# Clamping nine weight pieces in PSUM, one unit's maximum later, and the first batch's value products on half rows

## The chip, the cores and the metric

One core of a Trainium2 chip runs the whole program. The metric is the device time of one execution in microseconds (us), the median of several runs. One of the runs is taken with the hardware profiler, and all rows below come from that execution. TensorE is called PE, VectorE DVE, ScalarE ACT, GpSimd POOL, and the queue that issues the transfers SP.

## The reference

The program computes an attention with 32 memory slots per head and then two expert layers, all in fp32:

```python
# batch 8, heads 8, seq 576, head_dim 64, n_mem 32
a    = softmax(phi, axis=slots)                      # (b, h, s, 32)
k_m  = einsum('bhsm,bhsd->bhmd', a, k)
v_m  = einsum('bhsm,bhsd->bhmd', a, v)
attn = softmax(q @ k_m.T / 8)                        # (b, h, s, 32)
x    = (attn @ v_m) as 4608 tokens x 512
h    = x @ w_in;  g = max(0.01*h, h);  x = g @ w_out             # w_in 512x2048, w_out 2048x512
y    = sigmoid(x @ w_gate) * (x @ w_val) @ w2_out                # 512x1536 twice, 1536x512
```

The first expert's weights w_in and w_out, and the second's, arrive as float64 words; the kernel turns each word into a float32 itself. "Piece" is 128 x 512 such words.

## The kernel before, in words

Since `x @ w_in` is `attn @ (v_m @ w_in)`, the kernel never forms x. For each batch it builds the product of v_m and w_in (tile `vw`), in eight blocks of 256 columns, split in a high and a low half for three-pass fp32 products. The main loop then runs over (batch, half of the tokens, block of 128 hidden columns): a "step". In a step i, in the order in which instructions are written for every engine (an order by hand, with in-order queues):

1. `fin`: the high part (`gh`, ACT) and the low part (`gl`, POOL, for a few steps of the list `gldve` DVE) of the activation of step i+1.
2. `m1_in` of step i+2 (L801): six products on PE into a bank `ps_h`, then the activation `gr` on ACT (L818).
3. The vector parts `v...` of the attention units that are due, interleaved in rounds with `tick`s. If a `vw` block was multiplied in step i-1, its split (`done`, ACT copy and DVE subtraction) comes in front.
4. The PE parts `t...` of the units.
5. If due (`vw0`: steps 2, 5, 8, 13, 20, 22), the PE products of one more `vw` block of batch 0 (`vw_block`, L760).
6. `m1_out` of step i (L824): twelve products into four banks `acc`.

A unit is half of a batch's heads (two per batch). Its parts run in a chain: v1 the slots' maximum over tokens (L472), t1 a PE transpose, v2 the maximum over it (tile `mx`), t2 a product that spreads it, v3 exp input, v4 sums, t4 `ps_kv` (k_m and v_m), v5 their scaling (r on DVE, then tile `e` on ACT, L580), t5 transposes, v6 the copy to `kvT` (ACT, L607), t8 scores, v8 transposes (DVE, L635), v9 to v11 the softmax and its split into `at_hi` and `at_lo`. The list `chain1` gives for each part its step, counted from the unit's start: units of batch 1 start at steps 1 and 13. All PE parts of units and of `vw` blocks share one pool of two PSUM banks, `ps_a`, used in turn; a bank is given out again when the instructions that read it are done. PSUM is full: four banks `acc`, two `ps_h`, two `ps_a`.

The weights of the first expert are converted by ticks. Tick n starts piece n-1 (`a`: y, k and the sign, three ACT instructions), adds for piece n-4 (`c`, POOL), clamps piece n-2 (`b`, DVE, L226), shifts and xors piece n-3 (`b2`, DVE, L234), and stores piece n-5 (`d`: for w_out a split by ACT and POOL). A block of w_in is two pieces. `y` has five SBUF buffers, `k` four. `done_until(n)` runs ticks until piece n has passed.

Before the loop a prologue, written as a list of groups, runs the two units of batch 0, the first maximum of the third unit (`v1.2`) and twelve ticks (`T`); then the first two `vw` blocks are multiplied and split one after the other. Unit 0 and 1 of batch 0 keep zeros in the other unit's 64 rows of `kvT` (their scale is a column of a mask), so `vw_block` multiplies all 128 rows and adds both units' columns in one bank. From batch 1 on `vw_pair` (L777) multiplies only the unit's own 64 rows, of two blocks at once, one bank per unit.

After the first expert (703 us) the second expert runs on PE without a break to the end.

Of the kernel before, what the change touches and what calls it, by code (L numbers as in the profile page):

```python
# [8 lines left out]
F32 = mybir.dt.float32  # L9
F32R = mybir.dt.float32r  # L10
I32 = mybir.dt.int32
# [6 lines left out]

SCHED = {'vw0': [2, 5, 8, 13, 20, 22],
# [5 lines left out]
 'ticks': [1, 1, 1, 1, 2, 1, 1, 2, 0, 1, 0, 1, 1, 2, 0, 0, 0, 1, 1, 1, 1, 1, 0, 0, 1, 0, 0, 0, 0, 0],  # L27
 'lopool': [0, 1, 2, 3, 4, 5, 6, 7, 8, 9, 10, 11, 12, 13, 14],
 'gldve': [3, 4, 6, 12, 26, 31],
 'upool': ['v10.1', 'v10.2', 'v10.3', 'v11.0', 'v11.1', 'v11.2', 'v11.3', 'v9.0', 'v9.2', 'v9.3'],  # L30
# [63 lines left out]
            'lq1': 0,  # L94
            'lq2': 1,
            'lq3': 2,
            'v1': -5,
            't1': -1,
            'v2': 0,
            't2': 1,  # L100
            'v3': 3,
            'v3e': 3,
            'v4': 4,
# [15 lines left out]
def tile_kernel(  # L119
# [13 lines left out]
    nc = tc.nc  # L133
    P = 128
    B, H, S, D = q.shape
    M = phi.shape[3]
# [6 lines left out]
    HG = 4  # L143
    NG = H // HG
# [4 lines left out]
    VB = 256  # L149
# [14 lines left out]
    cvp = p1.enter_context(tc.tile_pool(name="cvp", bufs=2))  # L164
    q, k, v, phi = (x.rearrange("b (h g) s d -> b g h s d", g=NG) for x in (q, k, v, phi))
    dr = ctx.enter_context(tc.tile_pool(name="dr", bufs=1, space=bass.MemoryType.DRAM))
    ps_acc = ctx.enter_context(tc.tile_pool(name="ps_acc", bufs=4, space=bass.MemoryType.PSUM))
# [11 lines left out]
    def f32(ap):  # L179
        return ap.bitcast(F32)  # L180

    def wtile(tag, shape, dt, name):
        return wp.tile(shape, dt, tag=tag, name=name, bufs=SLOTS[tag])

    def split(raw, hi, lo, eng=nc.vector):
        nc.scalar.copy(hi, raw)  # L186
        eng.tensor_sub(lo, raw, f32(hi))  # L187
# [7 lines left out]
    PC = 512  # L195

    class Piece:
        late = False

        def __init__(self, src, done, f_dst=None, raw=None):  # L200
            self.src, self.done, self.f_dst, self.raw = src, done, f_dst, raw
# [7 lines left out]

        def a(self):  # L210
            w = self.raw.rearrange("p (n t) -> p n t", t=2)
            self.y = cvp.tile([P, PC], F32, tag="y", name="y", bufs=5)
            self.k = cvp.tile([P, PC], F32, tag="k", name="k", bufs=4)
            nc.scalar.activation(self.y, w[:, :, 1].bitcast(F32), AF.Abs, scale=2.0 ** -3)
            nc.scalar.activation(self.k, w[:, :, 0], AF.Copy, scale=2.0 ** -27, bias=2.0 ** 25)
            if not self.late:
                self.sign()
            yield
# [11 lines left out]

        def b2(self):
            w = self.raw.rearrange("p (n t) -> p n t", t=2)
            yi = self.y.bitcast(I32)
            nc.vector.scalar_tensor_tensor(  # L234
                out=yi, in0=yi, scalar=3, in1=w[:, :, 1].bitcast(I32),
                op0=ALU.logical_shift_left, op1=ALU.bitwise_xor,
            )
            yield
# [10 lines left out]
    win = {}  # L249
# [24 lines left out]
    def wout_pieces(j):  # L274
        def done(c, f):
            if c == 0:
                stage["wo", j] = [wtile("wo", [P, 2, DM], F32R, "wo") for _ in range(2)]
            hi, lo = (t[:, c, :] for t in stage["wo", j])
            split(f, hi, lo, nc.gpsimd if 2 * j + c in SCHED["lopool"] else nc.vector)
            wout[2 * j + c] = (hi, lo)  # L280
# [6 lines left out]
    def stash_jobs():  # L287
# [12 lines left out]
        def prep(key, o0):  # L300
# [40 lines left out]
            def h(f, *a):  # L341
                return lambda: f(*a)
# [51 lines left out]
    kvT = {}  # L394
    vw = {}
# [68 lines left out]
    def unit_engine(part, u):  # L464
        return nc.gpsimd if u[0] > 1 or f"{part}.{u[0] * NG + u[1]}" in SCHED["upool"] else nc.vector

    def psa(name):
        return ps_a.tile([P, 512], F32, tag="a", name=name)
# [288 lines left out]
            PARTS[n + "ab"[i]] = lambda u, f=f, i=i: f(u, i)  # L757


    def vw_block(j):  # L760
        p = psa("ps_vw")
        for g in range(NG):
            for h in range(HG):
                nc.tensor.matmul(
                    p[M * h:M * h + M, g * VB:(g + 1) * VB],
                    kvT[0, g][:, 1, M * h:M * h + M], win[j][:, h, :], start=True, stop=True,
                )

        def done():
            t = vw[0, j] = wtile("vw", [P, 2, NG, VB], F32R, "vw")  # L770
            split(p.rearrange("p (g f) -> p g f", g=NG), t[:, 0], t[:, 1])
            yield

        return done


    def vw_pair(b, j0):  # L777
        js = (j0, j0 + 1)
        ps = [psa("ps_vw") for _ in range(NG)]
        for n, j in enumerate(js):  # L780
            for h in range(HG):
                for g in range(NG):
                    nc.tensor.matmul(  # L783
                        ps[g][M * h:M * h + M, n * VB:(n + 1) * VB],
                        kvT[b, g][D * g:D * g + D, 1, M * h:M * h + M],
                        win[j][D * g:D * g + D, h, :], start=True, stop=True,
                    )
        for j in js:
            vw[b, j] = wtile("vw", [P, 2, NG, VB], F32R, "vw")
        for g in range(NG):  # L790
            ws = [(ps[g][:, n * VB:(n + 1) * VB], vw[b, j]) for n, j in enumerate(js)]
            for x, w in ws:
                nc.scalar.copy(w[:, 0, g], x)
            for x, w in ws:
                nc.vector.tensor_sub(w[:, 1, g], x, f32(w[:, 0, g]))  # L795

    hps = {}
    gt = {}
    acc = {}

    def m1_in(b, hf, fc):  # L801
# [17 lines left out]
        gt[b, hf, fc] = (gh, gl)  # L819
        return lambda: split(gr, gh, gl, nc.vector if b == 0 and hf * NF + fc in SCHED["gldve"] else nc.gpsimd)  # L820

    BEGIN = [sum(SCHED["groups"][:i]) for i in range(len(SCHED["groups"]) + 1)]

# [264 lines left out]
    with tc.manual_schedule():  # L1088
# [8 lines left out]
        pieces = []  # L1097
        pos = [0]
        for j in range(NVB):
            pieces += win_pieces(j) + wout_pieces(j)  # L1100
        n_start = len(pieces)

        raws = iter(pieces)

# [8 lines left out]
        def run(gens):  # L1113
            gens = list(gens)
            while gens:
                gens = [g for g in gens if next(g, gens) is not gens]

        def chain(gens):
            for g in gens:
                yield from g  # L1120
# [30 lines left out]
        def done_until(n):  # L1151
            while pos[0] < n + 5:
                run([tick()])
# [3 lines left out]

        U0 = dict(zip(units[2:], SCHED["units"]))
        for b in range(3, B):
            for g in range(NG):  # L1160
                U0[b, g] = (b - 1) * NS + SCHED["unit"][g]
        VW_AT = {b: [(b - 1) * NS + x for x in SCHED["vw"]] for b in range(3, B)}
# [13 lines left out]
        def first_vw(j):  # L1176
            done_until(4 * j + 2)
            return vw_block(j)

        def unit_parts(i):  # L1180
            vs, ts_, ls = [], [], []
            for u, u0 in U0.items():
                parts = [n for n, k in SCHED[{1: "chain1", 2: "chain2"}.get(u[0], "chain")].items() if k == i - u0]
                v = [PARTS[n](u) for n in parts if n[0] == "v"]
                if v:
                    vs.append(chain(v))
                ts_ += [(PARTS[n], u) for n in parts if n[0] == "t"]
                ls += [
                    (PARTS[n], u) for n in parts
                    if n[0] == "l" and u not in units[:3]  # L1190
                ]
            return vs, ts_, ls
# [6 lines left out]
            else:  # L1199
                (unit_phi, unit_kv, unit_q)["pkq".index(x[0])](units[int(x[1])])  # L1200
        waiting = []
        n_vw = n_in = 0
        fin = None
        for group in SCHED["prologue"]:
            vs, ts_ = {}, []
            for n, f in enumerate(waiting):
                vs["w", n] = [f()]
            waiting = []
            for x in group.split():
                if x == "T":  # L1210
                    vs.setdefault("T", []).append(tick())
                elif x == "W":
                    ts_.append(None)
                else:
                    n, u = x.split(".")
                    u = units[int(u)]
                    if n[0] == "v":
                        vs.setdefault(u, []).append(PARTS[n](u))
                    else:
                        ts_.append((PARTS[n], u))  # L1220
            run([chain(v) for v in vs.values()])
            for t in ts_:
                if t:
                    t[0](t[1])
                else:
                    waiting.append(first_vw(n_vw))
                    n_vw += 1
        run([f() for f in waiting])
        while n_vw < 2:
            run([first_vw(n_vw)()])  # L1230
            n_vw += 1
        for i in range(LA):
            fin = step_in(*steps[i])
            if i + 1 < LA:
# [67 lines left out]
        for n in range(len(PAIRS)):  # L1302
            more = n + 1 < len(PAIRS)
            for th in range(NTH):
                for j in range(TH // 2):
                    for val in range(2):
                        g = m2_group(n, th, j, val)
                        if (n, th, j, val) == (0, 0, 0, 0):
                            g = first
# [49 lines left out]
```

## Time and profile before

| what | value |
|---|---|
| device time, median of 3 runs | 1602.17 us (1600.76 to 8618.76) |
| the profiled execution's own time | 1601.75 us |
| its span, first to last instruction | 1599.9 us |
| PE busy | 1549.1 us, 97% |
| DVE, ACT, POOL busy | 827.7, 707.9, 431.0 us |
| mean granted clock of PE | 0.989 |

The span is 1.85 us shorter than the time of the same execution. Busy shares are means over the span; in the slices of the page PE shows 5 to 7 tenths in the first two of forty slices (40 us each) and 9 in nearly all others. The changed code runs in the first 145 us.

### The profile page before, as it was taken

The numbers are of one execution on the slowest core, as the hardware profiler recorded it, in microseconds if no ns is written. First come the engines' busy times: TensorE is split into PE (matmuls) and PEld (weight loads), VectorE is DVE, ScalarE is ACT, GpSimd is POOL, SyncE is SP. The second block draws the span as 40 slices with busy tenths as digits, with TensorE's granted clock in tenths as the row PEclk, the third lists the DMA queues.
The fourth block names the chain that finished last, engine by engine and source line by source line (L and its number), as shares of the span: only waits on it lengthen the run. The fifth ranks groups of instructions, "written<-read, shape, count | busy, mean of one in ns | idle before, by whom it ended". The sixth has DMA issues, their size and how long they took to land.

```text
span 1599.9 us, 27447 instructions
## 1 busy us (share of the span) xinstructions
PE 1549.1 (97%) x10544; PEld 1358.0 (85%) x10544; DVE 827.7 (52%) x1426; ACT 707.9 (44%) x1602; POOL 431.0 (27%) x429
## 2 busy tenths in 40 slices
PE   5799999999999999999999999999999999999998
PEld 2677988999999998999988888888888888888898
DVE  6886444555554545422145474355545475255544
ACT  5885455565556555645333143223333143223332
POOL 3886343554445444543100020000200020000100
PEclk8799999999999999999999999999999999999999
DMA  9822554554556455322446446536546446536692
GB/s 306 277 53 64 160 143 138 150 154 139 159 146 192 140 160 146 115 82 97 146 170 218 140 156 234 191 115 222 195 163 222 141 150 236 169 109 223 223 398 76
DMA packets 203490, 268.66 MB, mean 168 GB/s; under 512 B 95072, under 2 KB 140128, under 8 KB 203360
## 3 DMA queue, kind: packets, MB, share of 16 engines
q1 hardware_dynamic: 203360, 266.92, 52.1%
q8 instruction: 83, 1.36, 0.4%
q14 instruction: 47, 0.39, 0.1%
HBM read 219.68 MB, written 47.19 MB: 167 GB/s over the span
## 4 chain that ended last, share of the span: by engine, by line
PE 82%; ACT 1%; DVE 1%; DMA 1%; issue 0%; POOL 0%; DVEq 0%; SPq 0%; ACTq 0%; POOLq 0%
PE acc L835 20%; PE oacc L1041 18%; PE ps_y L943 14%; PE ps_h L813 9%; PE ps_x L943 9%; PE ps_z L943 9%; PE ps_vw L783 1%; PE ps_kv L550 1%; DMA wt<-gvs 1%; PE ps_sc L625 0%; ACT gr L818 0%; ACT obuf L844 0%; DVE vw L795 0%; DVE t L530 0%; ACT raw L222 0%
## 5 line engine op out<-in xcount | busy, mean ns | idle before, releaser
L835 PE MATMUL acc<-gh,wo 128*128 128x288 f32 x2048 | 428.7, 301 | 3.7 <-ACT obuf L844 2.7
L835 PEld LDWEIGHTS acc<-gh,wo 128*128 128x128 f32 x2048 | 328.9, 189 | 28.4 <-issue 13.8
L835 PE MATMUL acc<-gl,wo 128*128 128x288 f32 x1024 | 304.8, 298 | 2.1 <-POOL gl L187 2.1
L187 POOL TENSOR_TENSOR gl<-gr,gh 128x288 fp32r<-128x288 f32 x250 | 215.6, 864 | 329.9 <-ACT gh L186 216.6
L1041 PE MATMUL oacc<-w2t,pt 128*128 128x512 f32 x1296 | 296.3, 389 | 0.0
L1041 PEld LDWEIGHTS oacc<-w2t,pt 128*128 128x128 f32 x1296 | 243.1, 188 | 50.3
L943 PE MATMUL ps_y<-xo,wt 128*128 128x512 f32 (+1 forms) x1080 | 251.9, 369 | 0.0
L813 PE MATMUL ps_h<-at_hi,vw 128*128 128x288 f32 x1024 | 214.6, 298 | 6.1 <-ACT vw L186 4.7
L943 PEld LDWEIGHTS ps_y<-xo,wt 128*128 128x128 f32 x1080 | 190.4, 188 | 33.8
L818 ACT ACTIVATE gr<-ps_h 128x288 f32<-128x288 f32 x256 | 105.7, 413 | 254.2 <-PE ps_h L813 226.1
L906 POOL TENSOR_TENSOR xo<-xr,xo 128x512 fp32r<-128x512 f32 (+1 forms) x16 | 23.0, 1460 | 671.0 <-ACT xo L902 671.0
L835 PEld LDWEIGHTS acc<-gl,wo 128*128 128x128 f32 x1024 | 193.7, 189 | 3.0 <-POOL gl L187 3.0
L813 PEld LDWEIGHTS ps_h<-at_hi,vw 128*128 128x128 f32 x1024 | 166.6, 190 | 7.5 <-ACT vw L186 5.6
L943 PE MATMUL ps_z<-xo,wt 128*128 128x512 f32 (+1 forms) x720 | 167.4, 368 | 0.6 <-DMA wt<-gvs 0.6
L943 PE MATMUL ps_x<-xo,wt 128*128 128x512 f32 (+1 forms) x720 | 167.5, 368 | 0.0
L813 PE MATMUL ps_h<-at_lo,vw 128*128 128x288 f32 x512 | 151.6, 296 | 0.0
L978 ACT CAST pt<-sg 128x512 fp32r<-128x512 f32 (+1 forms) x120 | 69.4, 578 | 182.0 <-DVE sg L971 182.0
L943 PEld LDWEIGHTS ps_z<-xo,wt 128*128 128x128 f32 x720 | 127.0, 189 | 23.1 <-DVE tmp L1024 0.7
L943 PEld LDWEIGHTS ps_x<-xo,wt 128*128 128x128 f32 x720 | 127.2, 188 | 22.9
L186 ACT CAST gh<-gr 128x288 fp32r<-128x288 f32 x256 | 111.8, 437 | 2.2
L813 PEld LDWEIGHTS ps_h<-at_lo,vw 128*128 128x128 f32 x512 | 97.2, 190 | 0.0
L990 ACT COPY tmp<-ps_x 128x512 f32<-128x512 f32 (+1 forms) x60 | 32.5, 542 | 136.6 <-PE ps_x L943 136.6
(171 smaller groups left out, 1719.0 us busy)
## 6 DMA issues: line engine op xcount, KB each, us to landing
wt<-gvs SPq DMA_DIRECT2D x210, 512.0 KB, 4.6
w2t<-w2s SPq DMA_DIRECT2D x60, 512.0 KB, 5.5
gvs<-hl SPq DMA_DIRECT2D x84, 256.0 KB, 2.4
x2s<-obuf SPq DMA_DIRECT2D x15, 576.0 KB, 3.7
win<-in_moe_w_in_dram SPq DMA_DIRECT2D x16, 512.0 KB, 9.8
wo_bits<-in_moe_w_out_dram SPq DMA_DIRECT2D x16, 512.0 KB, 10.4
xr<-x2s SPq DMA_DIRECT2D x16, 512.0 KB, 6.2
out_dram<-osum SPq DMA_DIRECT2D x32, 256.0 KB, 2.0
```

The costliest lines, as they stand in the source:

```text
L186: nc.scalar.copy(hi, raw)
L187: eng.tensor_sub(lo, raw, f32(hi))
L550: nc.tensor.matmul(p[M * h:M * h + M, 0:2 * D], a, x, start=(c == 0), stop=(c == CC))
L783: nc.tensor.matmul(ps[g][M * h:M * h + M, n * VB:(n + 1) * VB], kvT[b, g][D * g:D * g + D, 1, M * h:M * h + M], win[j][D * g:D * g + D, h, ...
L813: nc.tensor.matmul(p[:, :HALF], w, x, start=(n == 0), stop=(n == 3 * NG - 1))
L818: nc.scalar.activation(gr, p[:, :HALF], AF.Prelu, alpha=0.01)
L835: nc.tensor.matmul(a[d][:, :HALF], w[:, ds_], x, start=(open_ and n == 0), stop=(close and n == 2),)
L906: eng.tensor_sub(t[:, 1, :h], x_operand(n, k, a), f32(t[:, 0, :h]))
L943: nc.tensor.matmul(bank, w[:, l, a, :], x[:, r, :h], start=(start and i == 0), stop=(i == 5), skip_group_check=not start,)
L978: nc.scalar.copy(d[:, 0, :h], s)
L990: read(lambda: nc.scalar.copy(s1, x))
L1041: nc.tensor.matmul(bank[i], pt[2 * f + t][:, l, q * P:(q + 1) * P], w2t[f][:, r, :], start=(f == 0 and l + r == 0), stop=(f == TH - 1 and ...
```

## The change

There are four edits. (1) For pieces 0 to 8 the tile y, which ACT writes and DVE clamps, lies in a PSUM bank of the `acc` pool; the shift and xor reads it there and writes an SBUF tile. (2) Part v1 of the third unit (batch 1, first half) leaves the prologue: in `chain1` v1 now has step -1 (of the unit's start at 1 and 13), and t1, v2 and t2 move one step later. (3) `vw_block` multiplies 64 rows per unit, as `vw_pair` does, into two banks of `ps_a`; its split is two ACT copies and two DVE subtractions of 256 columns in place of one each of 512. (4) The first two blocks are multiplied together at `W`, before the last prologue group, and their split runs interleaved with that group. The block of step 13 moves to step 12.

```diff
-SCHED = {'vw0': [2, 5, 8, 13, 20, 22],
+SCHED = {'vw0': [2, 5, 8, 12, 20, 22],
...
-              'v9.0 v7a.1 T v4.1 v9e.0 t4.1', 't7b.1 T', 't5.1 v5.1 v7b.1', 'T v1.2', 'v10.0 T', 't8a.1 v6.1',
-              'v10t.0 t8b.1 T v8a.1', 'v11.0', 'v8b.1 v9.1 T', 'T T v9e.1 T v10.1 v10t.1 v11.1'],
+              'v9.0 v7a.1 T v4.1 v9e.0 t4.1', 't7b.1 T', 't5.1 v5.1 v7b.1', 'T', 'v10.0 T', 't8a.1 v6.1',
+              'v10t.0 t8b.1 T v8a.1', 'v11.0', 'v8b.1 v9.1 T', 'T T v9e.1 W', 'T v10.1 v10t.1 v11.1'],
+ 'banks': 9,
...
-            'v1': -5,
-            't1': -1,
-            'v2': 0,
-            't2': 1,
+            'v1': -1,
+            't1': 0,
+            'v2': 1,
+            't2': 2,
...
         def a(self):
-            self.y = cvp.tile([P, PC], F32, tag="y", name="y", bufs=5)
+            if self.bank:
+                self.y = ps_acc.tile([P, PC], F32, tag="acc", name="y_bank")
+            else:
+                self.y = cvp.tile([P, PC], F32, tag="y", name="y", bufs=5)
...
         def b2(self):
-            yi = self.y.bitcast(I32)
+            y = self.y
+            if self.bank:
+                self.y = cvp.tile([P, PC], F32, tag="y", name="y", bufs=5)
             nc.vector.scalar_tensor_tensor(
-                out=yi, in0=yi, scalar=3, in1=w[:, :, 1].bitcast(I32),
+                out=self.y.bitcast(I32), in0=y.bitcast(I32), scalar=3, in1=w[:, :, 1].bitcast(I32),
...
+    def vw_products(b, js):
         ps = [psa("ps_vw") for _ in range(NG)]
         for n, j in enumerate(js):
             for h in range(HG):
                 for g in range(NG):
                     nc.tensor.matmul(
                         ps[g][M * h:M * h + M, n * VB:(n + 1) * VB],
                         kvT[b, g][D * g:D * g + D, 1, M * h:M * h + M],
                         win[j][D * g:D * g + D, h, :], start=True, stop=True,
                     )
+        return ps
...
+    def vw_block(j):
+        ps = vw_products(0, (j,))
+        def done():
+            vw_tiles(0, (j,))
+            for part in ("hi", "lo"):
+                vw_split(part, 0, [(0, j)], ps, range(NG))
+                yield
+        return done
...
+        def first_vws():
+            done_until(6)
+            ps = vw_products(0, (0, 1))
+            def done():
+                vw_tiles(0, (0, 1))
+                for j in (0, 1):
+                    for part in ("hi", "lo"):
+                        vw_split(part, 0, [(j, j)], ps, range(NG))
+                        yield
+            return done
```

## Rows read from the trace of the kernel before

**Rows 1.** Stretches: start:end length, then busy PE PEld DVE ACT POOL, clock, DMA
```profile
40.00:50.00 10.00, 2.54 (x16) 0.71 (x16) 9.93 (x13) 7.01 (x13) 7.21 (x7) 0.60 1.06 371
80.00:90.00 10.00, 9.46 (x112) 7.69 (x110) 9.86 (x12) 8.45 (x19) 8.18 (x8) 1.00 0.54 135
400.00:1600.00 1200.00, 1192.15 (x7301) 1041.29 (x7299) 583.33 (x990) 461.20 (x1007) 214.09 (x217) 1.00 0.52 171
```

**Rows 2.** Timeline, end of the prologue: start, duration, engine, line, tiles, [idle before]
```profile
52.10 0.61 PE L813 MATMUL ps_h<-at_hi,vw 128*128 128x288 f32 x1 [0.70 <-DVE vw L187]
52.54 0.79 POOL L187 TENSOR_TENSOR at_lo<-atr,at_hi 128x288 fp32r<-128x288 f32 x1
```

**Rows 3.** Timeline of DVE and POOL in the prologue
```profile
31.74 0.41 DVE L226 TENSOR_SCALAR y<-y 128x512 f32<-128x512 f32 x1
50.86 1.72 POOL L187 TENSOR_TENSOR wo<-y,wo 128x512 fp32r<-128x512 f32 x1
51.37 1.28 DVE L187 TENSOR_TENSOR vw<-ps_vw,vw 128x512 fp32r<-128x512 f32 x2
```

**Rows 4.** DVE in 20 to 53 us, L226 alone, then L234 alone
```profile
20.00:53.00 33.00, 8.17 (x11) 0.68 1.07 366
...
20.00:53.00 33.00, 9.39 (x9) 0.68 1.07 366
```

**Rows 5.** Timeline of PE: products of a block, of a pair, and what follows
```profile
61.28 1.19 PE L764 MATMUL ps_vw<-win,kvT 128*32 128x256 f32 x16
62.40 0.54 PE L835 MATMUL acc<-gh,wo 128*128 128x288 f32 x2
227.20 1.09 PE L783 MATMUL ps_vw<-win,kvT 64*32 64x256 f32 x32
228.23 0.54 PE L835 MATMUL acc<-gh,wo 128*128 128x288 f32 x2
```

**Rows 6.** Timeline and stretches: a pair held at a bank, and the clock then
```profile
239.47 1.50 PE L783 MATMUL ps_vw<-win,kvT 64*32 64x256 f32 x30 [3.08 <-DVE mx L492]
...
241.00:243.00 2.00, 2.00 (x9) 2.00 (x10) 1.32 (x4) 1.52 (x5) 0.34 (x1) 0.50 0.80 261
```

**Rows 7.** Timeline, steps 2 to 4: DVE's `gl`, and PE's wait for `obuf`
```profile
63.04 1.30 DVE L187 TENSOR_TENSOR gl<-gr,gh 128x288 fp32r<-128x288 f32 x1 [0.18 <-ACT gh L186]
70.20 0.85 PE L835 MATMUL acc<-gh,wo 128*128 128x288 f32 x2 [2.73 <-ACT obuf L844]
```

**Rows 8.** Timeline, step 8: PE's block, DVE's r, ACT's scaling
```profile
85.46 1.53 PE L764 MATMUL ps_vw<-win,kvT 128*32 128x256 f32 x16
88.89 0.15 DVE L560 TENSOR_SCALAR r<-ps_kv 128x1 f32<-128x1 f32 x1
88.95 1.09 DVE L479 TENSOR_REDUCE t<-ph 128x128 f32<-128x512 f32 x1
90.16 0.47 ACT L580 ACTIVATE e<-ps_kv,r 128x256 f32<-128x256 f32 x1 [1.14 <-DVE r L562]
```

**Rows 9.** Timeline, step 23: the split in front of a PE part
```profile
138.11 0.41 ACT L818 ACTIVATE gr<-ps_h 128x288 f32<-128x288 f32 x1 [2.63 <-PE ps_h L813]
139.78 0.71 PE L625 MATMUL ps_sc<-qT,kvT 64*32 64x288 f32 x14 [1.16 <-DVE vw L187]
```

**Rows 10.** Timeline, steps 12 and 20: PE, and what a block there waits for
```profile
99.45 0.51 PE L835 MATMUL acc<-gh,wo 128*128 128x288 f32 x2
101.25 1.72 POOL L242 TENSOR_TENSOR win<-y,k 128x512 int32<-128x512 int32 x1
126.13 1.07 PE L764 MATMUL ps_vw<-win,kvT 128*32 128x256 f32 x16
130.15 0.45 ACT L580 ACTIVATE e<-ps_kv,r 128x256 f32<-128x256 f32 x1
```

**Rows 11.** Waits in 50 to 145 us: who for whom: us in total, times, longest
```profile
PE acc L835 <- POOL gl L187: 2.1, 3, 1.1
PE ps_kvT L595 <- ACT e L580: 1.4, 2, 0.9
```

More of the change, by code (lines that the diff above doesn't have):

```diff
@@ L197, in tile_kernel @@
     class Piece:
-        late = False
+        late = bank = False
         def __init__(self, src, done, f_dst=None, raw=None):
@@ L757, in tile_kernel @@
             PARTS[n + "ab"[i]] = lambda u, f=f, i=i: f(u, i)
[L760 to L778, printed above, removed]
+    def vw_products(b, js):
         ps = [psa("ps_vw") for _ in range(NG)]
@@ L787, in vw_pair, with vw_split, vw_tiles @@
                     )
+        return ps
+    def vw_split(part, b, js, ps, gs):
+        for g in gs:
+            for n, j in js:
+                x, w = ps[g][:, n * VB:(n + 1) * VB], vw[b, j]
+                if part == "hi":
+                    nc.scalar.copy(w[:, 0, g], x)
+                else:
+                    nc.vector.tensor_sub(w[:, 1, g], x, f32(w[:, 0, g]))
+    def vw_tiles(b, js):
         for j in js:
             vw[b, j] = wtile("vw", [P, 2, NG, VB], F32R, "vw")
-        for g in range(NG):
[L791 to L795, printed above, removed]
+    def vw_block(j):
[6 more added lines that the diff above has]
+        return done
+    def vw_pair(b, j0):
+        js = (j0, j0 + 1)
+        ps = vw_products(b, js)
+        vw_tiles(b, js)
+        for g in range(NG):
+            for part in ("hi", "lo"):
+                vw_split(part, b, list(enumerate(js)), ps, (g,))
     hps = {}
@@ L1101, in tile_kernel @@
         n_start = len(pieces)
+        for p in pieces[:SCHED["banks"]]:
+            p.bank = True
         raws = iter(pieces)
@@ L1178, in first_vw @@
             return vw_block(j)
+        def first_vws():
[4 more added lines that the diff above has]
+                for j in (0, 1):
+                    for part in ("hi", "lo"):
+                        vw_split(part, 0, [(j, j)], ps, range(NG))
+                        yield
+            return done
         def unit_parts(i):
@@ L1201, in tile_kernel @@
         waiting = []
-        n_vw = n_in = 0
         fin = None
@@ L1225, in tile_kernel @@
                 else:
[L1226 to L1231, printed above, removed]
+                    waiting.append(first_vws())
         for i in range(LA):
```

## The prediction

> **What bounds the kernel now.** I first read the stretches of the span [rows 1]. After 400 us PE is busy 1192 of 1200 us and nothing of the change runs there, so only the first 145 us can move. There two regimes follow each other. In 40 to 50 us DVE is busy 9.93 of 10 and PE 2.54 at a clock of 0.60: DVE sets the time at which PE can start the main loop. In 80 to 90 us PE is busy 9.46, but DVE 9.86: PE leads and DVE follows some microseconds behind, which costs nothing as long as PE has other work in front of what DVE owes it. Next I read the timeline at the border of the two [rows 2]: the first product in full flow starts at 52.10 (PE had waited for a low half from DVE), and POOL's last `at_lo` of the prologue, which the same products need, runs from 52.54. Then I read the waits of PE in the loop [rows 7, 11]: 2.73 us at 70.20 for `obuf`, 2.1 in three for POOL's `gl`, 1.4 in two for `e`. These are the waits that another delay of PE would swallow.
>
> **The prologue (edits 1, 2 and the pair).** DVE loses the maximum of the third unit, 1.09 by its like at 88.95 [rows 8], and its small second instruction: 1.3 us. It moves to step 0, where DVE waits for ACT before its next clamp; if that cover is gone it costs the same 1.3. The nine shift-and-xors take 9.39 us in all, 1.04 each [rows 4]. A subtraction of the same size with one operand in PSUM took 0.64 while POOL worked beside it (51.37, POOL from 50.86) [rows 3]; at that price nine cost 5.8, a gain of 3.6. The clamps: eleven take 8.17 [rows 4], so nine about 6.7, in proportion. No row shows a clamp in PSUM. One end is 0.41, the clamp in SBUF beside no POOL work [rows 3], nine for 3.7; the other is 0.64, nine for 5.8. I take 0.64, since its operand lies in PSUM as the changed clamp's does: a gain of 0.9 (at the other end 3.0). The Trainium skill, "VectorE: DVE Perf Modes", section "Why PSUM operands drop a tier", speaks against this edit: an fp32 operand in PSUM keeps DVE from its two-port mode. By that rule the clamp costs one element per cycle and the sum stays as it is; without it DVE would gain 2.1 us more.
>
> ACT's nine writes of y into PSUM have no row either. I take nothing, between one clamp's difference of 0.23 gained and as much lost for each.
>
> DVE is thus about 5.8 us shorter. What is late next is POOL: its queue keeps its order, and a store (1.72) and the multiplication of the softmax stand ahead of `at_lo` [rows 2, 3]. The new order even puts both splits and one more tick ahead of unit 1's sums on DVE. So between 0 and 5.8 I take **-2.0**: POOL's row at 52.54 lies close behind PE's release at 52.10, nearer to no gain than to all. The pair itself runs while PE has nothing else to do: 0. Transfers are issued in the same order: 0.
>
> **Products on half rows (edit 3).** An undisturbed block takes 61.28 to 62.40, 1.12; a pair of half-row blocks 227.20 to 228.23, 1.03, so 0.52 a block [rows 5]. Six blocks lie in the loop: 6 x 0.6 = **-3.6** (at least -2.4, if one block alone does not pipeline as a pair does and costs 0.72). The split in two costs ACT and DVE one fixed cost more each, which ACT's and DVE's idle time after 94 us hides; before that it counts in the lags below.
>
> **What edit 3 adds: two banks instead of one.** `ps_a` has two. A block now waits until both are read, and the unit's PE part of the next step waits until the block is split. PE is in order, so everything behind stands still. A pair shows this wait already: 3.08 us until DVE's maximum `mx`, and then a clock of 0.50, the lower of its two levels, for at least 2 us, which loses 1.0 us [rows 6].
> - Step 2: v2 now falls in this step, and DVE runs it behind `gl`, which ends at 64.34; with the maximum (0.3, estimated) 64.6. PE is there at 61.28: +3.3 [rows 5, 7].
> - Step 3: t2 waits for the split, which ACT runs behind the `gr` of the product that PE has just made. In step 23 the same order already costs 138.11 to 139.78, 1.67, of which 1.16 is idle [rows 9]; with halves of 256 columns I take +1.3. The wait at 70.20 is then paid: -2.73. Clock: one drop before and one after, 0.
> - Step 5: its readers ran a step earlier, 0.
> - Step 8: `e` ends at 90.63; without the other unit's maximum, which now is due in step 12, r's second instruction follows the first and `e` ends near 89.7. PE is there at 85.46 [rows 8]: 4.2, less 0.7 by which PE is late by then (3.3 + 1.3 - 2.73 - two blocks' 1.2): +3.5. The clock after it: +1.0. The later wait of t5 for the same `e` goes: -0.5 [rows 11].
> - Steps 9 and 13: the split in front of t5 and t1, +1.3 each.
> - Step 12: the block waits for a conversion that ends at 102.97, and stands where PE was at 99.45 [rows 10]: 3.5, but PE is 5.4 late by then, so 0.
> - The waits for `gl`: -2.1 [rows 11].
> - Step 20: `e` ends at 130.60, PE was there at 126.13 [rows 10]: 4.5; PE is 4.0 late: +0.5. Its t5's own wait: -0.9.
> - Step 21: +1.3. Steps 22 and 23 already have theirs: 0.
>
> Sum: 3.3 + 1.3 - 2.7 + 3.5 + 1.0 - 0.5 + 1.3 + 1.3 - 2.1 + 0.5 - 0.9 + 1.3 = +7.3. With -2.0 and -3.6: **+1.7 us**. Against the profiled execution's 1601.75 this is 1603.5; the median of the runs shown lies 0.4 above it, so I leave it at 1603.5.
>
> **Rivals.** *The gain is kept (0.30).* DVE, freed of POOL, keeps its lead into the loop, so that the readers of steps 2 and 8 come early. Then the start gives -4, the blocks -3.6, the two waits about 1 each, the four splits 5.2, and half of the 6.2 us of old waits is swallowed: -3.5, 1598. For it: DVE ends the prologue with little idle time [rows 1]. Against: what DVE follows at step 2 is ACT's `gh` (0.18 idle before 63.04 [rows 7]), and ACT loses no work.
>
> *The waits pile up, slower (0.15).* My zeros in steps 12 and 20 assume that the other engines do not wait for PE. But ACT's queue in each step stands behind the `gr` of a product that PE has just made, so when PE is late the reader may be as late. Then steps 12 and 20 pay their 3.5 and 4.5 in full with a clock drop each: +3.5 + 4.0 + 2.0 more, 1613. It decides from the point at which PE idles over 2 us ahead of the block's products in step 12. The Trainium skill, "TensorEngine Tiling (Array Packing)", section "Restrictions and Gotchas", names its root: different row tiles write to different banks, so row tiling raises the pressure on PSUM. No run here shows yet what that costs a single block.
>
> *The first edits do nothing (0.05):* POOL holds the start where it is. Then +3.7, 1605.5.
>
> My forecast, even within some microseconds (1599 to 1607), has 0.50.
>
> **The numbers.** 1595 to 1611 leaves out the ends of the two large rivals, about 0.2. The forecast's own range is 1599 to 1607. 2%, about what a measurement of this kernel can tell from no change, is 32 us. No case reaches that: all PE waits of the first 60 us together would be needed for a gain, and three times the pile-up for a loss. So faster 0.01, same 0.97, slower 0.02.
>
> **What would show it.** Start: the first product in full flow near 50, not 52.1; shift-and-xor of the first nine pieces at 0.64 whatever POOL does; clamps at 0.64. Blocks: 0.5 to 0.6 of PE each. Waits: idle time of PE ahead of the block's products in step 2 (for `mx`) and step 8 (for `e`), some 3 us each, with the clock at 0.50 behind, and 1 us ahead of t2, t5 and t1; no wait at `obuf`. I am wrong if PE reaches the products of step 8 with `e` already done (faster), or if step 12 or 20 idles as long as step 8 (slower).

## The result and the profile after

The changed kernel takes 1619.34 us (median of 4 runs, 1616.80 to 1620.36), against 1601.74 for the kernel before in the same runs: ratio 1.0110, 95% interval 1.0090 to 1.0129. It is slower by about 1.1%, and above the range given. The profiled execution took 1616.80, 15.05 more than that of before (1601.75); its span is 1615.0.

| | before | after |
|---|---|---|
| span, us | 1599.9 | 1615.0 |
| PE busy, us | 1549.1 | 1551.4 |
| DVE, ACT, POOL busy, us | 827.7, 707.9, 431.0 | 818.8, 708.0, 428.2 |
| mean granted clock of PE | 0.989 | 0.987 |

DVE is indeed relieved of 9 us and PE works nearly as long as before: the loss is idle time of PE. The stretches that answer to [rows 1] (start:end length, busy PE, PEld, DVE, ACT, POOL, clock, DMA):

```profile
40.00:50.00 10.00, 3.46 (x19) 1.18 (x19) 7.12 (x14) 6.89 (x14) 7.75 (x7) 0.50 1.06 374
80.00:90.00 10.00, 5.63 (x77) 4.43 (x75) 8.39 (x12) 8.80 (x21) 8.52 (x7) 1.00 0.59 141
400.00:1600.00 1200.00, 1195.29 (x7391) 1045.72 (x7390) 586.99 (x992) 466.11 (x1022) 220.53 (x224) 1.00 0.52 171
```

In 80 to 90 us PE falls from 9.46 to 5.63. After 400 us PE is about as busy as before. The waits of PE in 50 to 145 us, which answer to [rows 11] (who for whom: us in total, times, longest):

```profile
PE ps_vw L771 <- ACT e L586: 7.1, 2, 4.8
PE ps_h L826 <- ACT at_hi L187: 5.2, 1, 5.2
PE ps_vw L771 <- POOL win L248: 3.4, 2, 2.7
PE ps_vw L771 <- DVE mx L498: 2.5, 1, 2.5
PE acc L848 <- POOL gl L188: 1.3, 1, 1.3
...
PE ps_vw L771 <- DVE e L641: 1.0, 2, 0.6
```

14.0 us of waiting now stand in front of the blocks' products (`ps_vw`), where before there were 0.4. Most of the single waits, from the timeline of PE (start, duration, tiles, [idle before <- releaser]):

```profile
64.07 0.66 PE L771 MATMUL ps_vw<-win,kvT 64*32 64x256 f32 x14 [2.50 <-DVE mx L498]
68.53 0.49 PE L507 MATMUL ps_m<-dg,ones 128*128 128x128 f32 x2 [1.22 <-DVE vw L785]
90.43 1.10 PE L771 MATMUL ps_vw<-win,kvT 64*32 64x256 f32 x14 [4.80 <-ACT e L586]
96.32 0.44 PE L601 MATMUL ps_kvT<-ident,e 128*128 128x128 f32 x2 [1.28 <-DVE vw L785]
106.36 0.63 PE L771 MATMUL ps_vw<-win,kvT 64*32 64x256 f32 x6 [0.63 <-DVE e L641]
109.64 0.64 PE L771 MATMUL ps_vw<-win,kvT 64*32 64x256 f32 x8 [2.65 <-POOL win L248]
115.61 0.33 PE L493 MATMUL ps_t<-ident,t 128*128 128x128 f32 x1 [1.22 <-DVE vw L785]
141.51 1.10 PE L771 MATMUL ps_vw<-win,kvT 64*32 64x256 f32 x14 [2.32 <-ACT e L586]
```

These are steps 2, 3, 8, 9, 12 (twice), 13 and 20. To see what each costs in the end, I took from both timelines the start of the first `m1_out` product of each step; the difference is how late the changed kernel is:

| first product of step | 0 | 2 | 3 | 5 | 8 | 9 to 11 | 12 | 13 | 16 | 20 | 21 | 23 |
|---|---|---|---|---|---|---|---|---|---|---|---|---|
| before, us | 56.09 | 62.40 | 64.90 | 76.47 | 87.53 | 90.88 | 99.45 | 104.01 | 112.89 | 127.13 | 130.85 | 140.42 |
| after, us | 55.84 | 64.66 | 68.77 | 75.70 | 91.46 | 96.52 | 110.20 | 115.69 | 127.02 | 142.54 | 147.65 | 156.58 |
| late by | -0.25 | 2.26 | 3.87 | -0.77 | 3.93 | 5.64 | 10.75 | 11.68 | 14.13 | 15.41 | 16.80 | 16.16 |

(The times under 9 to 11 are step 9's.) The fall from step 3 to step 5 is the old wait for `obuf` [rows 7], which is gone, and the low clock behind it, which is gone too: before, PE's clock was 0.50 from 70 to 72 us, and it needed 6.27 us from step 4 to step 5, now 4.46. After step 21 the delay shrinks for a while: the third store of `x2s` is issued at 210.95 before and 226.93 after (16.0), the fourth at 261.81 and 275.31 (13.5), because a pair of batch 1 that waited 3.08 us and then ran at the low clock [rows 6] now waits 1.98, and its products behind the wait take 1.09 us, not 1.50:

```profile
254.46 1.09 PE L771 MATMUL ps_vw<-win,kvT 64*32 64x256 f32 x30 [1.98 <-DVE mx L498]
```

Up to the ninth store it stays near 13.2 (486.39 and 499.55), and at the tenth it is 15.2 (529.47 and 544.64): in between, ACT waited 4.08 us for a weight's transfer (up to 530.11) and PE 0.52 and 0.76 us for DVE. So about 2 us of this execution's loss come after 400 us, where a transfer landed late. (The first expert ends later than is said further up: in the kernel before its last product starts at 787.6.)

### The profile page after: what moved, and what is told of

Read it like the earlier page. It is cut to its first block, busy times and chain, and to the rows that moved or that the text cites. A ratio compares the mean times of both kernels' runs of the same rounds, so it can differ in the third digit from the quotient of the medians.

```text
span 1615.0 us, 27469 instructions
## 1 busy us (share of the span) xinstructions
PE 1551.4 (96%) x10544; PEld 1358.7 (84%) x10544; DVE 818.8 (51%) x1434; ACT 708.0 (44%) x1610; POOL 428.2 (27%) x429
## 4 chain that ended last, share of the span: by engine, by line
PE 79%; DMA 2%; ACT 2%; DVE 1%; issue 1%; SPq 0%; POOL 0%; DVEq 0%; ACTq 0%; POOLq 0%
PE oacc L1054 18%; PE acc L848 18%; PE ps_y L956 14%; PE ps_x L956 9%; PE ps_z L956 9%; PE ps_h L826 9%; PE ps_vw L771 1%; PE ps_kv L556 1%; DMA kv<-in_k_dram 1%; DMA wt<-gvs 0%; PE ps_sc L631 0%; DMA raw<-in_moe_w_gate_dram 0%; DMA ph<-in_phi_dram 0%; ACT gr L831 0%; DVE vw L785 0%
## 5 line engine op out<-in xcount | busy, mean ns | idle before, releaser
L785 DVE TENSOR_TENSOR vw<-ps_vw,vw 128x256 fp32r<-128x256 f32 x128 | 45.8, 418 | 113.9 <-ACT vw L783 113.8
```

## The experiments

The kernels ran beside the kernel before, in three sets in which that took 1600.99, 1602.89 and 1602.80 us; every ratio is to the one of its own set. After the result my theory was: two banks per block in the loop cost nearly all of it, because PE then waits for readers that do not get ahead of it; the prologue gains nothing because its new order undoes what the clamps free. Rivals: the products on 64 rows themselves, the split's four small instructions, the order of the first pair, or the block moved to step 12.

### Which edit: 128 rows in one bank again, and 128 rows in two banks

`full_rows` gives the blocks of the loop back their old form; the start and the schedule stay as in the changed kernel (diff shortened).

```diff
     def vw_block(j):
-        ps = vw_products(0, (j,))
+        p = psa("ps_vw")
+        ... 16 products of 128 rows into p, split as before
```

> The changed kernel with one thing undone: the single blocks of the loop multiply all 128 rows into one bank again; the pair at W, the clamps in PSUM and the later maximum stay. Theory 'two banks': the 17 us come from PE standing in front of a block's products until both banks are read, and in front of the next step's unit part until the block is split, with clock drops behind. Then this returns to 1599 to 1604 us, and the waits of PE for mx, e (4.8 us in step 8) and the split are gone. Rival 'start': the pair and its split ahead of unit 1's softmax, and what follows from it, cost the time. Then it stays above 1612.

Measured: 1607.28, ratio 1.0040 [1.0025, 1.0055]. Most of the loss is gone, but 0.4% stays, more than I allowed for. The trace shows where (PE's products, then POOL's conversion that they wait for):

```profile
102.91 1.92 PE L795 MATMUL ps_vw<-win,kvT 128*32 128x256 f32 x12 [4.27 <-POOL win L248]
```
```profile
99.67 3.18 POOL L248 TENSOR_TENSOR win<-y,k 128x512 int32<-128x512 int32 x1
```

Even with one bank, the block at step 12 comes 4.27 us before its weights, and after that wait PE runs at a granted clock of 0.50 from 104 to 108 us. Up to step 11 this kernel was 1.5 us ahead of the one before; with step 12 it was 5.3 behind. (It was 10.0 behind at step 16, 7.6 at step 23, and 5.5 after batch 1's pair.)

`full_rows_two_banks` has the rows of before and the banks of after (diff shortened):

```diff
-  kvT[b, g][D * g:D * g + D, 1, M * h:M * h + M], win[j][D * g:D * g + D, h, :],
+  kvT[b, g][:, 1, M * h:M * h + M], win[j][:, h, :],      # single blocks only
```

> The changed kernel, but a single block of the loop multiplies all 128 rows (the other unit's rows are zeros) into two banks: the half-row saving is given up and the two banks are kept. Theory 'two banks': as slow as the changed kernel and up to 4 us more, 1618 to 1624 us, since PE waits for the same readers. Rival 'half rows': products on 64 rows are themselves what disturbs PE; then this returns to about 1603.

Measured: 1618.16, 1.0109 [1.0094, 1.0124], no different from the changed kernel, with its waits (PE, steps 8 and 12):

```profile
90.39 1.95 PE L771 MATMUL ps_vw<-win,kvT 128*32 128x256 f32 x14 [4.70 <-ACT e L586]
...
110.17 1.34 PE L771 MATMUL ps_vw<-win,kvT 128*32 128x256 f32 x8 [2.21 <-POOL win L248]
```

So it is the second bank, not the rows: taking it away gains 0.7%, and half the rows in the same two banks gain nothing. `full_rows` also takes back the split in four small instructions, but these cost little by themselves: ACT's two copies of 256 columns take 0.64 us against 0.59 for the one of 512, DVE's two subtractions 0.76 (at 95.84) against 0.69 (at 91.78). ACT before, then after:

```profile
91.16 0.59 ACT L186 CAST vw<-ps_vw 128x512 fp32r<-128x512 f32 x1
```
```profile
95.44 0.64 ACT L783 CAST vw<-ps_vw 128x256 fp32r<-128x256 f32 x2
```

### The start: edit 1 alone, the old order, the pair alone

`banks_only` is the kernel before with the nine clamps in PSUM and nothing else (beside the lines of edit 1 in `a` and `b2`, shown under the change):

```diff
+        for p in pieces[:9]:
+            p.bank = True
```

> The kernel before with edit 1 alone. Theory: the clamps and shift-and-xors of nine pieces take 0.60 us each start to start, free of POOL, which gives most of the 3.5 us by which the first products in full flow come earlier with edits 1 and 2: start near 49 us, 1599 to 1601 us. Rival: the maximum is what counts (1.3 us of DVE ahead of unit 1's chain): no change, 1602.

Measured: 1599.84, 0.9985 [0.9976, 0.9995]. The products start 3.1 us earlier than the 52.10 of [rows 2]. POOL's multiplication of the softmax runs 1.3 us earlier (45.50, before 46.84), DVE's transposes behind it and ACT's first copy of the split 1.8 us (46.70 and 48.40, before 48.47 and 50.16), and the second wait of before, for DVE's low half at 52.10, is gone. PE, then POOL:

```profile
49.03 1.33 PE L818 MATMUL ps_h<-at_hi,vw 128*128 128x288 f32 x2 [3.48 <-ACT vw L186]
```
```profile
45.50 1.16 POOL L720 TENSOR_TENSOR unit_a<-unit_a,st 128x576 f32<-128x576 f32 x1 [0.50 <-ACT y L217]
```

`pair_last` is the changed kernel with the pair multiplied and split after the softmax of unit 1 (diff shortened):

```diff
-  'v8b.1 v9.1 T', 'T T v9e.1 W', 'T v10.1 v10t.1 v11.1'],
+  'v8b.1 v9.1 T', 'T T v9e.1 T v10.1 v10t.1 v11.1', 'W'],
```

> The changed kernel with the pair of the first two blocks multiplied and split after the last prologue group, as before, not ahead of unit 1's softmax. Theory: in the changed kernel the splits and a store stand ahead of POOL's multiplication (49.50 against 46.84 us before), which eats what DVE saves by the clamps in PSUM; here the first product in full flow comes about 2 us earlier than at 52.6, but the waits in the loop remain: 1616 to 1619 us. Rival 'start': the order in the prologue is the main cost; then this is at 1608 or below.

Measured: 1616.59, 1.0101 [1.0084, 1.0118]. The start is won and then lost again: the first products run at 47.91, 4.2 us before [rows 2], but the steps with two banks take it back (2.85 in step 2, 4.88 in step 8).

```profile
47.91 1.07 PE L826 MATMUL ps_h<-at_hi,vw 128*128 128x288 f32 x2 [3.38 <-ACT vw L783]
```

A lead of PE over its readers is used up at the blocks that wait for them: against the changed kernel it is 3.4 us in step 0, 2.1 in step 8 and 0.1 in step 20. `pair_first` is the kernel before with edit 4's order alone:

```diff
-  'v10t.0 t8b.1 T v8a.1', 'v11.0', 'v8b.1 v9.1 T', 'T T v9e.1 T v10.1 v10t.1 v11.1'],
+  'v10t.0 t8b.1 T v8a.1', 'v11.0', 'v8b.1 v9.1 T', 'T T v9e.1 W', 'T v10.1 v10t.1 v11.1'],
```

> The kernel before with edit 4 alone: the first two blocks as a pair on half rows at W, split interleaved with the last prologue group. No clamps in PSUM, old maximum, single blocks as before. Theory: the splits, a store and a tick stand ahead of the softmax of unit 1, so the first products in full flow come 1 to 3 us later than 52.10, and the time is 1602 to 1605 us. Rival: the split was the last thing PE waited for (0.70 us at 52.10), so having it early gains 1 us: 1600.

Measured: 1603.03, 1.0001 [0.9991, 1.0010]: no change. Its full flow starts at 53.33, 1.2 later than before:

```profile
53.33 0.85 PE L831 MATMUL ps_h<-at_hi,vw 128*128 128x288 f32 x2 [3.89 <-ACT at_hi L187]
```

### Edits 1 and 2, then with 4, and the block's step

`later_max` (edit 2 alone on the kernel before, diff shortened):

```diff
-  'T v1.2', ...        'v1': -5, 't1': -1, 'v2': 0, 't2': 1,
+  'T', ...             'v1': -1, 't1': 0,  'v2': 1, 't2': 2,
```

> The kernel before with edit 2 alone: the third unit's maximum in step 0, t1, v2 and t2 a step later, and so the other unit's in step 12. Theory: 1.3 us less DVE work in the prologue, start near 51 us, 1601 to 1602 us of 1602. Rival: t2's later place makes PE wait for dg in step 3 (up to 1 us), so 1603.

Measured: 1602.37, 0.9997 [0.9987, 1.0007], no change. `banks_and_max` is edits 1 and 2 together, with the diffs shown:

> The kernel before with edits 1 and 2 alone: nine clamps in PSUM and the later maximum (with t1, v2, t2 a step later); blocks on 128 rows in one bank, at the old steps, the first two after the softmax. Theory: the products in full flow start near 48 us, as they do in the changed kernel with the pair last (47.91), against 52.10 before; part of the 4 us is lost again where PE waits for obuf, so 1597 to 1600 us. Rival: DVE sets the first 94 us, the start is given back whole: 1600 to 1602.

Measured: 1599.63, 0.9980 [0.9970, 0.9989]. This is faster than both kernels, by 0.2% and (0.9980 / 1.0110) 1.3%; from `banks_only` it can't be told apart. `full_rows_13` adds edit 4's order, the blocks in one bank at their old steps, which is `full_rows` with one number changed:

```diff
-SCHED = {'vw0': [2, 5, 8, 12, 20, 22],
+SCHED = {'vw0': [2, 5, 8, 13, 20, 22],
```

> The changed kernel with the single blocks on 128 rows in one bank and the block of step 12 back in step 13. In the run with that block in step 12 PE waited 4.27 us there for a conversion (tick for piece 21), and the clock fell behind it. Theory 'two banks, and step 12 for the conversion': that wait goes, 1600 to 1603 us. Rival 'start': the prologue order keeps 4 us or more of loss, 1605 to 1608.

Measured: 1604.03, 1.0007 [0.9997, 1.0016]. Against `full_rows` the block's step is worth 0.33%; against `banks_and_max` edit 4's order costs 0.27%, all of the gain of the clamps. In its profiled execution, the slowest of its ten, 2.4 us are there from step 0 on, and some 4 us more come only at batch 1's pair (step 57), where PE waits 3.91 us for `mx` at 242.32; why that pair does worse here was not followed. Its full flow begins at 51.83, as in the changed kernel, 3.2 us after that of `banks_and_max`:

```profile
51.83 0.85 PE L831 MATMUL ps_h<-at_hi,vw 128*128 128x288 f32 x2 [5.22 <-ACT at_hi L187]
```
```profile
48.60 1.33 PE L818 MATMUL ps_h<-at_hi,vw 128*128 128x288 f32 x2 [2.75 <-ACT vw L186]
```

### Can the waits be moved away?

`tick_earlier` is the changed kernel with one tick of step 13 moved to step 10, so that the conversion that step 12 waits for runs earlier.

```diff
-  'ticks': [1, 1, 1, 1, 2, 1, 1, 2, 0, 1, 0, 1, 1, 2, 0, ...
+  'ticks': [1, 1, 1, 1, 2, 1, 1, 2, 0, 1, 1, 1, 1, 1, 0, ...
```

> The changed kernel with one of step 13's two ticks moved to step 10, so that the conversion that the block of step 12 needs is issued in step 11. Theory: the wait of 2.65 us in step 12 goes and about 1 us of low clock behind it; the others stay: 1614 to 1617 us. Rival 'serial conversions': DVE and POOL are as late with the tick in step 10, so the wait only moves: 1618 to 1620.

Measured: 1617.11, 1.0088 [1.0073, 1.0103]; the interval overlaps the changed kernel's. The 2.65 us in step 12 are gone: PE starts that step's `m1_out` 7.7 us late instead of 10.8, and that of step 16 5.8 instead of 14.1. But step 20 then waits 3.89 in place of 2.32, and batch 1's pair 3.91 in place of 1.98:

```profile
106.53 0.66 PE L771 MATMUL ps_vw<-win,kvT 64*32 64x256 f32 x14 [0.63 <-DVE e L641]
...
137.04 0.66 PE L771 MATMUL ps_vw<-win,kvT 64*32 64x256 f32 x14 [3.89 <-ACT e L586]
...
252.75 1.95 PE L771 MATMUL ps_vw<-win,kvT 64*32 64x256 f32 x30 [3.91 <-DVE mx L498]
```

The fourth store of `x2s` is issued at 275.70, no earlier than the changed kernel's 275.31. `split_at_once` lets the readers of a block run in the block's own step:

```diff
-                held = first_vw(VW_AT[0][i])
+                run([first_vw(VW_AT[0][i])()])
```

> The changed kernel with each single block split in the step of its products, ahead of that step's second product group, not in the next step behind the next activation. Theory 'two banks': the waits in front of the next step's unit part (1.2 to 1.3 us each in steps 3, 9, 13, 21, 23) go, 6 us in all; the waits for readers stay (2.5, 4.8, 2.7, 2.3): 1611 to 1615 us. Rival: the waits only move to the readers, whose engines now run the split first: no change, 1617 to 1620.

Measured: 1613.49, 1.0082 [1.0067, 1.0097]. All five waits of 1.2 to 1.3 for `vw` are gone. Steps 8 and 20 wait longer for `e` (5.33 and 3.34, not 4.80 and 2.32); in step 8 `e` starts 0.8 us later (90.69, in the changed kernel 89.90), behind DVE's r, which is as much later:

```profile
91.22 1.10 PE L771 MATMUL ps_vw<-win,kvT 64*32 64x256 f32 x14 [5.33 <-ACT e L586]
```

`blocks_moved` takes the blocks out of the steps in which they wait for `e`:

```diff
-SCHED = {'vw0': [2, 5, 8, 12, 20, 22],
+SCHED = {'vw0': [2, 5, 10, 12, 17, 22],
```

> The changed kernel with two of its blocks in other steps: the one of step 8 goes to step 10, where the bank's reader is ACT's short copy to kvT, and the one of step 20 to step 17, where the readers ran a step earlier and no unit part follows. Theory 'readers in the same step': the waits of 4.8 and 2.3 us for e, the low clock behind each (1.3 and 1.0 us) and the split wait of step 21 go; a wait for the split stays in front of the part of step 11: 1607 to 1612 us. Rival 'two banks anywhere': the time just moves to the next place where DVE and ACT are late, 1616 or more.

Measured: 1614.19, 1.0069 [1.0051, 1.0086]. It lies between the changed kernel and the 1607 to 1612 that I had expected. Both waits for `e` are gone, and two others stand there: 3.06 us in step 8 for a bank of `acc` that ACT copies out (`pbuf`), and 3.51 in step 17 for a conversion:

```profile
89.50 0.85 PE L848 MATMUL acc<-gh,wo 128*128 128x288 f32 x2 [3.06 <-ACT pbuf L857]
...
130.17 1.08 PE L771 MATMUL ps_vw<-win,kvT 64*32 64x256 f32 x8 [3.51 <-POOL win L248]
```

The first was there in the kernel before too, 0.54 long, behind the block of step 8. `quiet_half` starts from `banks_and_max` and gives the half-row form only to the blocks of steps 5 and 20, the latter moved to step 17:

```diff
-SCHED = {'vw0': [2, 5, 8, 13, 20, 22],
+SCHED = {'vw0': [2, 5, 8, 13, 17, 22],
...
-            return vw_block(j)
+            return (vw_half if j in (3, 6) else vw_block)(j)   # vw_half: 64 rows, two banks
```

> The kernel before with edits 1 and 2 (run as banks and max at 0.998 of before) and half-row products in two banks only for two blocks whose banks have no reader in the same step and no unit part in the next: the one of step 5, and that of step 20 moved to step 17. Theory: each of the two saves about 0.5 us of PE and waits for nothing new: 0.997 to 0.9985 of before. Rival: the earlier conversions that step 17 asks for hold PE as in step 12 of the changed kernel: 1.000 or more.

Measured: 1605.26, 1.0020 [1.0010, 1.0031], slower than the kernel it starts from. In step 17 PE waits 1.45 and 4.41 us and then runs at the lower clock (PE; then a stretch of it):

```profile
114.05 0.63 PE L786 MATMUL ps_vw<-win,kvT 64*32 64x256 f32 x6 [1.45 <-DVE pht L523]
119.08 1.08 PE L786 MATMUL ps_vw<-win,kvT 64*32 64x256 f32 x8 [4.41 <-POOL win L247]
```
```profile
120.00:122.00 2.00, 2.00 (x12) 1.91 (x9) 0.00 (x0) 0.60 (x2) 1.54 (x3) 0.50 0.00 0
```

The half-row block of step 5 did what was hoped: from step 4 to step 5 the kernel gains 1.6 us on the one before, `banks_and_max` 1.2. The loss lies in steps 17 and 18, and most of it is a conversion asked for too early; half rows in step 5 alone were not run. So no schedule tried here made the second bank pay. A third bank for `ps_a` might take the wait away; PSUM is full, and it was not tried.

## Why the prediction was wrong

The step that failed is the one on **step 12**: "3.5, but PE is 5.4 late by then, so 0", and with it "PE is 4.0 late: +0.5" in step 20. The lateness itself came out: 5.64 us in steps 9 to 11. That it would cover the wait was wrong. It holds only if the engine that PE waits for goes on while PE is late. It did not. ACT's activation stood behind a product of the late PE, DVE's split behind ACT (4.04 us of idle time ahead of 95.84), and POOL and DVE behind PE's products (ACT, POOL, DVE after; then POOL and DVE before):

```profile
95.13 0.41 ACT L831 ACTIVATE gr<-ps_h 128x288 f32<-128x288 f32 x1 [4.43 <-PE ps_h L826]
```
```profile
98.43 1.28 POOL L188 TENSOR_TENSOR wo<-y,wo 128x512 fp32r<-128x512 f32 x1 [6.95 <-PE acc L848]
...
106.39 3.19 POOL L248 TENSOR_TENSOR win<-y,k 128x512 int32<-128x512 int32 x1
```
```profile
102.85 1.65 DVE L855 TENSOR_TENSOR obuf<-acc,obuf 128x288 f32<-128x288 f32 x4 [4.38 <-PE acc L848]
```
```profile
94.08 1.41 POOL L187 TENSOR_TENSOR wo<-y,wo 128x512 fp32r<-128x512 f32 x1 [3.22 <-PE ps_h L813]
```
```profile
97.21 1.65 DVE L842 TENSOR_TENSOR obuf<-acc,obuf 128x288 f32<-128x288 f32 x4 [2.87 <-PE acc L835]
```

POOL idled 6.95 us there instead of 3.22 and DVE 4.38 instead of 2.87; ACT had not waited for that product at all (its `gr` at 90.85 before). The conversion that step 12 needs ended at 109.58 instead of 102.97 [rows 10], 6.6 later, with PE 5.6 late: it began 5.1 later and took 3.19 us instead of 1.72, while DVE's clamps and shifts ran from 106.51 to 108.46. So step 12 paid 0.35 + 0.63 + 2.65 = 3.6 us where I had put 0, and step 20 paid 2.32.

Not all of the 3.6 is that mechanism. The 0.35 and 0.63 are waits for DVE's transposes `e`, between which DVE runs the maximum that edit 2 put into this step (104.81, 1.01 long); before, both transposes ran together (98.78). And the 1.5 us by which the conversion took longer have no tested cause: in `full_rows`, where PE was not late, it took 3.18 as well. With 1.72 it would have ended 5.1 later, and by these rows (an estimate) some 2.2 of the 3.6 would have stayed.

After these waits PE ran at a lower clock, as the stretches behind the waits of steps 8, 12 and 20 show (columns as above):

```profile
92.00:94.00 2.00, 2.00 (x12) 2.00 (x11) 0.00 (x0) 0.00 (x0) 0.00 (x0) 0.62 0.47 75
112.00:114.00 2.00, 2.00 (x10) 2.00 (x10) 0.00 (x0) 0.00 (x0) 2.00 (x3) 0.50 0.00 0
142.00:144.00 2.00, 2.00 (x20) 1.46 (x7) 1.30 (x2) 0.30 (x1) 1.89 (x2) 0.50 0.62 70
```

The first row also shows the others standing behind PE: from 92 to 94 us PE is the only engine that works. That is the rival "the waits pile up", with 0.15, down to its reason (ACT's queue behind `gr`) and its point of decision (PE idle over 2 us ahead of the products of step 12). Its 1613 was still 3.8 too low for the profiled execution; 1.75 of that is the 2.0 of the start, which it kept.

The sum, against the 15.05 measured:

| part | predicted | measured | from |
|---|---|---|---|
| start | -2.0 | -0.25 | step 0 of the table |
| steps 2 to 11 | +5.4 | +5.89 | 5.64 + 0.25 |
| steps 12 to 23 | -1.7 | +10.52 | 16.16 - 5.64 |
| later | 0 | -1.1 | 15.05 - 16.16 |

Of the 13.35 us that were missed, 12.2 lie in steps 12 to 23, 1.75 in the start, 0.5 in steps 2 to 11 and -1.1 later. Of the 12.2, 5.3 lie in steps 12 and 13, 3.6 in steps 14 to 16 (the waits for `gh` and `gl`, below) and 3.8 in steps 20 and 21, with 0.5 gained elsewhere. That steps 2 to 11 came out within 0.5 is partly luck: the low clock behind the old wait for `obuf`, which went without a new one in its place, and the wait of step 8, which was longer, cancel.

- *Clamps and shifts: right.* Nine clamps in PSUM took 0.685 each (0.64 taken), nine shifts 0.675 whatever POOL did (0.64 taken), where [rows 4] had 1.04. By operation, minimum, median and maximum in ns:

```profile
L230 DVE TENSOR_SCALAR y_bank<-y_bank x9: 666/685/693, 20.6 to 42.3; 128x512 f32<-128x512 f32 x9
L218 ACT ACTIVATE y_bank<-win x5: 630/646/672, 13.6 to 39.1; 128x512 f32<-128x512 f32 x5
L240 DVE SCALAR_TENSOR_TENSOR y<-y_bank,win x5: 671/676/683, 25.7 to 46.2; 128x512 int32<-128x512 int32 x5
```

  The clamp bears out the Trainium skill, "VectorE: DVE Perf Modes", section "Why PSUM operands drop a tier", by which an fp32 operand in PSUM leaves DVE at one element per cycle: 0.685 here against the 0.41 of a clamp in SBUF [rows 3]. The shift agrees with the Trainium skill, "SBUF — State Buffer", section "Who interferes with whom", by which DVE contends with a POOL instruction that reads SBUF when both of DVE's inputs lie there, and with one, outside the two-port modes, does not: 671 to 683 ns here, 674 to 1765 for the same five before.

- *The start: right for edit 1, wrong for the sum.* The clamps bring 2 to 3 us (`banks_only`, first product of step 0 at 2.03 us earlier). Edit 4 takes them: the splits of the pair go ahead of the high half of a w_out piece on ACT, so POOL's store waits 2.25 us, and the softmax's multiplication stands behind the store. I had named that order and still kept -2.0. One line per link, over ACT, POOL, DVE and PE:

```profile
47.49 0.66 ACT L187 CAST wo<-y 128x512 fp32r<-128x512 f32 x1
48.28 1.26 POOL L188 TENSOR_TENSOR wo<-y,wo 128x512 fp32r<-128x512 f32 x1 [2.25 <-DVE vw L785]
49.50 1.16 POOL L721 TENSOR_TENSOR unit_a<-unit_a,st 128x576 f32<-128x576 f32 x1
50.69 0.84 DVE L736 STREAM_TRANSPOSE atr<-unit_a 128x288 f32<-128x288 f32 x2 [2.54 <-POOL unit_a L721]
51.20 0.79 ACT L187 CAST at_hi<-atr 128x288 fp32r<-128x288 f32 x2 [3.05 <-DVE atr L736]
51.69 0.85 PE L826 MATMUL ps_h<-at_hi,vw 128*128 128x288 f32 x2 [5.21 <-ACT at_hi L187]
```

- *Steps 2, 3, 9 and 13: the waits right, one clock term wrong.* 2.50 for `mx` (3.3 predicted), 1.22, 1.28 and 1.22 for the splits (1.3 each); the wait for `obuf` is gone. But "Clock: one drop before and one after, 0" failed: the drop behind `obuf` went, and none came behind step 2, so that PE was 0.8 us early in step 5.
- *Step 8: right in kind, too small.* 4.80 where 3.5 was taken: PE was not late by 0.7 but early by 0.4 (85.02 against 85.46), and `e` ended at 90.37, not near 89.7. The low clock behind it cost about 1.4 (0.44 in the block's 14 products, 0.93 in `m1_out`), not 1.0.
- *The waits for `gl`: wrong on the whole.* Of the three that were to be swallowed (-2.1), those of 0.41 and 0.58 in steps 18 and 19 went. In step 15 the 1.10 became 0.83 for `gh` and 1.31 for `gl`, with a clock of 0.56 behind (124 to 126 us). DVE had idled 6.01 us ahead of the split at 115.13, behind ACT.
- *Half rows: the price right, the gain nothing.* 14 products in 0.66 us at full clock against 1.09 on 128 rows (`full_rows_two_banks`); with PE waiting inside the block and behind it, no run shows a gain.

The forecast of no change within 2% held. That two banks, not rows, cost 0.7%, that the block's step costs 0.33% with one bank and edit 4 with edits 1 and 2 0.27% is shown by runs. That the three add up to the whole (0.9980, 1.0007, 1.0040, 1.0110) is read across sets that did not share a chip run. The changed kernel with nothing but its block back in step 13 was not run, so what that step costs with two banks is open.

## What to carry to other kernels

A wait is not paid for by an earlier wait unless the engine waited for runs on meanwhile: look in the trace whether its queue has work that does not stand behind the late engine, and if it is idle behind it, charge both waits. In an in-order queue a second buffer per result costs nothing while it is free and a full stall when its reader is late; count the buffers that a change holds before the time its instructions save. Where several edits come together, run each alone: here one of four was worth 0.15% by itself, and the others hid it.

## What the runs showed of the hardware

A clock drop did not follow every wait: after 2.50 us of idle PE ahead of 64.07 the granted clock stayed at 1.00, the upper of its two levels, in the next 2 us; after the 4.80 and 2.32 ahead of 90.43 and 141.51 it fell to 0.53 (nearly all of it the lower level, 0.50) and 0.50, and in the kernel before, after the 2.73 ahead of 70.20, to 0.50. Ahead of 64.07 and of 70.20 PE had run at full clock from about 56 us on, ahead of 141.51 from about 128 us on. What tells the cases apart no run here shows. The stretches right behind the waits of steps 2 and 8, in the changed kernel:

```profile
64.00:66.00 2.00, 1.93 (x24) 1.52 (x25) 1.95 (x4) 1.61 (x4) 1.55 (x2) 1.00 1.05 402
...
90.00:92.00 2.00, 1.57 (x16) 0.76 (x17) 1.07 (x1) 0.70 (x2) 1.48 (x2) 0.53 0.46 72
```

ACT wrote y to PSUM about as fast as to SBUF: for w_in 646 ns (median of five) against 642 and 672 in two later pieces, for w_out 664 (median of four) against 675 and 693.
